# The last microseconds of a one-core decode kernel: output sum turned to five rows, contiguous weight reads, six pieces for the last load

## Chip, cores, metric

The kernel runs on one core of one Trainium2 chip. The metric is the device time of one execution in microseconds (us), as the median of several executions. The profile is one execution taken by the hardware profiler. Its engines are PE (matmul; PEld is its weight load), DVE (VectorE), ACT (ScalarE), POOL and SP. SP mostly issues DMAs here. "L395" is line 395 of that kernel's file.

## The reference

One token passes a layernorm, then attention over a cache of 32 heads x 32768 positions x 128, plus, in parallel, a SwiGLU feed-forward block. All is added to the input:

```python
x  = A_x                                        # [1, 1, 640] bf16
xn = layernorm(x)
return x + attention(xn, k_cache, v_cache, wq, wo) + (silu(xn @ w_gate) * (xn @ w_up)) @ w_down
# k_cache, v_cache: [1, 32, 32768, 128] bf16; wq [640, 4096]; wo [4096, 640]; w_down [1728, 640]
```

The two caches are 537 MB of the 554 MB that the kernel reads.

## The kernel before

SP streams everything through a ring of three SBUF slots: wq, then K and V of each head, then the feed-forward weights, and last wo. At the end PE forms `w_down` and `wo` products in one PSUM tile `acc` of 128 partitions x 5 columns, DVE adds the input, and SP writes 640 values out. These are the parts that the change touches:

```python
D = 640; NCD = 5; OC = 32                      # 32 row blocks of wo, one per 128 rows
WTAIL = [16, 8, 4, 2, 2]                       # row blocks per wo load, a semaphore each
...
wd_v = wd.rearrange("p j (m c) -> p j m c", c=NCD)            # output column = 5*m + c
wo_v = wo.rearrange("p (j m c) -> p j m c", j=OC, c=NCD)
...
# SP, after all K and V, and the feed-forward weights
for i, n in enumerate(WTAIL):
    e.dma_start(wo[:, j * D:(j + n) * D], wo_src[:, j * D:(j + n) * D]).then_inc(s_wo[i], 16)
    j += n
e.wait_ge(s_fin, 1)
e.dma_start(out[0, 0:1, :].rearrange("o (p c) -> (o p) c", c=NCD), outb[:, :]).then_inc(s_out, 16)
...
# PE
def project():
    j = 0
    for i, n in enumerate(WTAIL):
        t.wait_ge(s_wo[i], 16)
        for _ in range(n):
            for c in range(NCD):
                mm = t.matmul(acc[:, c:c + 1], lhsT=wo_v[:, j, :, c], rhs=ot[:, j:j + 1], ...)
            j += 1
...
# DVE
v.wait_ge(s_att, 1)
v.tensor_tensor(out=outb[:, :], in0=xf[:, :], in1=acc, op=ALU.add).then_inc(s_fin, 1)
```

For each row block, five matmuls of one moving column each use a 128x128 piece of the weight as the stationary operand. Column `c` of `acc` holds outputs `5*m + c`, so a weight load reads every fifth element (10 bytes apart), and partition `m` of `outb` holds five neighbouring outputs. The output DMA is therefore 128 runs of 10 bytes.

Of the kernel before, what the change touches and what calls it, by code (L numbers as in the profile page):

```python
# [5 lines left out]
ALU = mybir.AluOpType  # L6
ACTF = mybir.ActivationFunctionType
AX = mybir.AxisListType
BF16 = mybir.dt.bfloat16
F32 = mybir.dt.float32  # L10


def bass_parallel_sum__gqa_block_cached__swiglu_ffn__decode_kernel(
# [18 lines left out]
    NCD = D // 128  # L32
# [14 lines left out]
    TAIL = [128, 64, 32, 32]  # L47
    RB = DH // 32
    OC = H * DH // 128
    WTAIL = [16, 8, 4, 2, 2]  # L50
    PARTS = [64, 64, 128]
    W = 512 // DH
    assert sum(TAIL) == NJ and sum(PARTS) == NJ and NHF == 4 and (H - H0) % PER == 0 and PER % SLOTS == 0
    assert PER % PR == 0 and PER % SR == 0
    assert OC == 32 and H * RB == 128 and sum(WTAIL) == OC
    HA = 5
# [22 lines left out]
    with ExitStack() as es:  # L79
        def sbt(name, shape, dtype):  # L80
            return es.enter_context(nc.sbuf_tensor(name, shape, dtype))

        def sem(name):
            return es.enter_context(nc.semaphore(name))
# [5 lines left out]
        ident = sbt("ident", [128, 128], BF16)  # L90
# [7 lines left out]
        ot = sbt("ot", [128, OC], BF16)  # L98
        hcol = sbt("hcol", [128, FB], BF16)
        sg = sbt("sg", [128, 2, FB], F32)  # L100
        one1 = sbt("one1", [1, 1], BF16)
        xf = sbt("xf", [128, NCD], F32)
        xc = sbt("xc", [128, NCD], F32)
        xq = sbt("xq", [128, NCD], F32)
        xn = sbt("xn", [128, NCD], BF16)
        outb = sbt("outb", [128, NCD], BF16)
# [8 lines left out]
        s_x, s_wq, s_out = sem("x"), sem("wq"), sem("o")  # L115
# [11 lines left out]
        s_exp, s_pv, s_o4, s_fold, s_ov = sem("exp"), sem("pv"), sem("o4"), sem("fold"), sem("ov")  # L127
        s_f, s_fa, s_fd = sem("ffn_pe"), sem("ffn_act"), sem("ffn_dve")
        s_att, s_fin = sem("att"), sem("fin")
        s_ob, s_op, s_ot = sem("o_blocks"), sem("o_ps"), sem("o_rows")  # L130
        block = es.enter_context(nc.Block())

# [3 lines left out]
        xrow = flat[0:1, x0 + NCD * 128:x0 + NCD * 128 + D]  # L136
# [8 lines left out]
        wd = flat[:, d0:d0 + FB * D].rearrange("p (j d) -> p j d", j=FB)  # L145
        assert 2 * NCD * F + FB * D <= CE
        wg_v = wg.rearrange("p (c n) -> p c n", c=NCD)
        wu_v = wu.rearrange("p (c n) -> p c n", c=NCD)
        wd_v = wd.rearrange("p j (m c) -> p j m c", c=NCD)

        def hidden(w, c, j):
            if j < FM:
                return w[:, c, 0:FM * 128].rearrange("p (m j) -> p m j", j=FM)[:, :, j]
            return w[:, c, FM * 128:F]
        wo = flat[:, WO_S * CE:WO_S * CE + OC * D]
        wo_v = wo.rearrange("p (j m c) -> p j m c", j=OC, c=NCD)
        assert OC * D <= CE

        def kv_src(cache, h, j0, n):
# [21 lines left out]
        with nc.psum_tensor("ps8", [128, 8, 512], F32) as ps8:  # L181
# [3 lines left out]
            op = ps8[:, 5, 8:8 + OC]  # L185
            acc = ps8[:, 6, 0:NCD]
            fold_ps = ps8[:, 6, 8:9]
            misc = ps8[:, 7, :]
            ffn = bank[0]

            @block.sync
            def sp(e):
                owner = {}
                for u in units:
                    s = slot_of[u]
                    if s in owner:
                        e.wait_ge(*owner.pop(s))
                    if u[0] == "wq":
                        e.dma_start(wq, A_wq.rearrange("(p c) n -> p (c n)", c=NCD)).then_inc(s_wq, 16)  # L199
                        owner[s] = (s_q, NQB)  # L200
                    elif u[0] == "k":
                        e.dma_start(ring[:, s, :], kv_src(A_k_cache, u[1], 0, NJ)).then_inc(s_slot[s], 16)
                        owner[s] = (s_qk, NHF * (u[1] + 1))
                    elif u == LASTV:
                        j = 0
                        for i, n in enumerate(TAIL):
                            e.dma_start(ring[:, s, j * DH:(j + n) * DH],
                                        kv_src(A_v_cache, u[1], j, n)).then_inc(s_tail[i], 16)
                            j += n
                    elif u[0] == "v":  # L210
                        e.dma_start(ring[:, s, :], kv_src(A_v_cache, u[1], 0, NJ)).then_inc(s_slot[s], 16)
                        owner[s] = (s_pv, u[1] + 1)
                    elif u[0] == "ffn":
                        e.dma_start(wg, B_w_gate.rearrange("(p c) n -> p (c n)", c=NCD)).then_inc(s_ffn[0], 16)
                        e.dma_start(wu, B_w_up.rearrange("(p c) n -> p (c n)", c=NCD)).then_inc(s_ffn[1], 16)
                        e.dma_start(flat[:, d0:d0 + FM * D], B_w_down[0:FM * 128, :].rearrange(
                            "(p j) n -> p (j n)", j=FM)).then_inc(s_ffn[2], 16)
                        e.dma_start(wd[0:FL, FM, :], B_w_down[FM * 128:F, :]).then_inc(s_ffn[2], 16)
                    else:
                        wo_src = A_wo.rearrange("(p j) n -> p (j n)", j=OC)  # L220
                        j = 0
                        for i, n in enumerate(WTAIL):
                            e.dma_start(wo[:, j * D:(j + n) * D], wo_src[:, j * D:(j + n) * D]).then_inc(s_wo[i], 16)
                            j += n
                e.wait_ge(s_fin, 1)
                e.dma_start(out[0, 0:1, :].rearrange("o (p c) -> (o p) c", c=NCD), outb[:, :]).then_inc(s_out, 16)
                e.wait_ge(s_out, 16)

            @block.gpsimd
# [21 lines left out]
            def pe(t):  # L251
# [2 lines left out]
                t.wait_ge(s_a, 2)  # L254
                for c in range(NCD):
                    mm = t.matmul(misc[:, 8 + c:9 + c], lhsT=xrow_v[:, :, c], rhs=one1[:, :], start=True, stop=True)
                mm.then_inc(s_pa, 1)

                t.wait_ge(s_a, 4)
# [6 lines left out]
                for b in range(NQB):  # L266
                    for c in range(NCD):
                        mm = t.matmul(bank[b], lhsT=xnb[:, c, :], rhs=wq_v[:, c, b * 512:(b + 1) * 512],  # L268
                                      start=(c == 0), stop=(c == NCD - 1))
# [108 lines left out]
                def down():  # L378
                    t.wait_ge(s_ffn[2], 32)
                    t.wait_ge(s_fd, 8)  # L380
                    first = True
                    for j in range(FB):
                        n = 128 if j < FM else FL
                        for c in range(NCD):
                            t.matmul(acc[:, c:c + 1], lhsT=wd_v[0:n, j, :, c], rhs=hcol[0:n, j:j + 1],
                                     start=first, stop=False, skip_group_check=True)
                            first = False

# [3 lines that stand above are left out]
                        t.wait_ge(s_wo[i], 16)  # L392
                        for _ in range(n):
                            for c in range(NCD):
                                mm = t.matmul(acc[:, c:c + 1], lhsT=wo_v[:, j, :, c], rhs=ot[:, j:j + 1],  # L395
                                              start=False, stop=(j == OC - 1), skip_group_check=True)
                            j += 1
                    return mm
# [17 lines left out]
                down()  # L416
                t.wait_ge(s_ot, 1)
                project().then_inc(s_att, 1)

            @block.scalar  # L420
            def act(a):
# [54 lines left out]
            def dve(v):  # L476
                n_a = [0]

                def step(ins):
                    ins.then_inc(s_a, 1)  # L480
                    n_a[0] += 1
                    v.wait_ge(s_a, n_a[0])
# [2 lines left out]
                step(v.memset(one1[:, :], 1.0))  # L485
                v.wait_ge(s_pa, 1)
                step(v.tensor_copy(out=xf[:, :], in_=misc[:, 8:8 + NCD]))
                step(v.tensor_reduce(out=st[:, 0:1], in_=xf[:, :], axis=AX.X, op=ALU.add))
                v.wait_ge(s_pa, 2)
                step(v.tensor_scalar(out=st[:, 1:2], in0=misc[:, 0:1], scalar1=1.0 / D, scalar2=None,  # L490
# [56 lines left out]
                with v.Fori(0, (H - H0) // PER) as i:  # L547
                    group[0] = i
                    for h in range(H0, H0 + PER):
# [11 lines left out]
                                in1=blk[:, None, :].to_broadcast([128, H, RB]), op=ALU.mult).then_inc(s_ob, 1)  # L561
                v.wait_ge(s_fa, 2)
                pieces = [(slice(0, 128), slice(0, FM)), (slice(0, FL), slice(FM, FB))]
                n = 0
                for stage in range(4):
                    for p, f in pieces:
                        fu = slice(FB + f.start, FB + f.stop)
                        if stage == 0:
                            ins = v.tensor_scalar(out=sg[p, 0, f], in0=sg[p, 0, f], scalar1=1.0, scalar2=None,
                                                  op0=ALU.add)  # L570
                        elif stage == 1:
                            ins = v.reciprocal(out=sg[p, 1, f], in_=sg[p, 0, f])
                        elif stage == 2:
                            ins = v.tensor_tensor(out=sg[p, 0, f], in0=sg[p, 1, f], in1=ffn[p, f], op=ALU.mult)
                        else:
                            ins = v.tensor_tensor(out=hcol[p, f], in0=sg[p, 0, f], in1=ffn[p, fu], op=ALU.mult)
                        ins.then_inc(s_fd, 1)
                        n += 1
                    v.wait_ge(s_fd, n)
                v.wait_ge(s_att, 1)  # L580
                v.tensor_tensor(out=outb[:, :], in0=xf[:, :], in1=acc, op=ALU.add).then_inc(s_fin, 1)


# [26 lines left out]
```

## Time and profile before

| what | value | where it is read |
|---|---|---|
| time, median of 3 runs at first | 1289.76 us (1289.53 to 1289.88) | the runs |
| span of the profiled run | 1288.2 us | the page |
| bytes, rate | 554.17 MB at 430 GB/s | the page, DMA line |
| PE, DVE busy | 81%, 52% of the span | the page |

The first view is from the page: DMA busy tenths and GB/s in 40 slices, and the sum of the packets.

```profile
DMA  9999999999999999999999999999999999999998
GB/s 421 426 425 446 426 429 442 429 431 440 431 431 433 435 431 429 440 431 431 440 427 431 444 427 431 442 429 431 435 433 433 429 438 433 427 442 431 427 422 340
DMA packets 11182, 554.17 MB, mean 430 GB/s; under 512 B 1377, under 2 KB 1442, under 8 KB 1826
```

DMA reads 9 everywhere but in the last slice. The kernel is bound by its stream of bytes, and no other engine's work can shorten the middle. What is left is what happens before the stream is under way and after its last byte. The timeline shows the end (start in us, duration, engine, line, operation, operands, count; in brackets the idle time before it and what ended it; the lines of PEld are left out, here and below):

```profile
1274.55 3.02 PE L385 MATMUL ps<-hcol,ring 128*128 128x1 bf16 x70 [1.49 <-DVE hcol L576]
...
1277.78 6.76 PE L395 MATMUL ps<-ot,ring 128*128 128x1 bf16 x160 [0.21 <-DMA ring<-in_A_wo_dram]
1284.65 0.16 DVE L581 TENSOR_TENSOR outb<-xf,ps 128x5 bf16<-128x5 f32 x1 [10.24 <-PE ps L395]
1284.84 0.35 SPq L226 DMA_DIRECT2D out_dram<-outb  x1
```

The 160 matmuls of wo (L395) look like one solid block after the first piece landed, 42 ns each. The DMA view gives, per issue, size and time from issue to landing:

```profile
ring<-in_A_wo_dram SPq DMA_DIRECT2D x1, 2560.0 KB, 25.2
ring<-in_A_wo_dram SPq DMA_DIRECT2D x1, 1280.0 KB, 28.1
ring<-in_A_wo_dram SPq DMA_DIRECT2D x1, 640.0 KB, 29.1
ring<-in_A_wo_dram SPq DMA_DIRECT2D x2, 320.0 KB, 29.6
...
out_dram<-outb SPq DMA_DIRECT2D x1, 1.2 KB, 3.0
```

With issues from 1252.43 on, the pieces landed at 1277.64, 1280.94, 1282.38, 1283.15 and 1283.94 us (single semaphore events of the trace). The stream itself ended at 1283.94. The program ended 4.27 us later, and 2.98 us of that is the output of 1.2 KB.

### The profile page before, as it was taken

Reading aid. Unit: us, or ns where it says so; the run is one execution under the profiler, and the core shown is the slowest. Engines: PE = TensorE matmul, PEld = TensorE weight load, DVE = VectorE, ACT = ScalarE, POOL = GpSimd, SP = SyncE. Lnnn points to the kernel's source line nnn. Section 1 sums busy time; section 2 is a strip of 40 time slices with the busy share of each in tenths; the row PEclk is TensorE's granted clock in tenths of the full one; section 3 lists DMA queues with packets and bytes.
Section 4 is the critical chain, followed back from the end, with each engine's and each line's share of the span. In section 5 each row is a group of like instructions: output and inputs, shape, how many; then the busy total and the mean of one; then the engine's idle time right before and its main releaser. Section 6 shows DMA issues by size and latency. Waiting matters only on the chain.

```text
span 1288.2 us, 9847 instructions
## 1 busy us (share of the span) xinstructions
PE 1043.7 (81%) x5148; PEld 263.9 (20%) x3228; DVE 670.0 (52%) x407; ACT 52.2 (4%) x140; POOL 2.5 (0%) x17
## 2 busy tenths in 40 slices
PE   4598778789777788778788777788777788777797
PEld 1011112221112221112221112221112221112237
DVE  0855665445665445664446664446664446664440
ACT  2000000000000000000000000000000000000000
POOL 0000000000000000000000000000000000000000
PEclk9799888898888999888898888898888998888895
DMA  9999999999999999999999999999999999999998
GB/s 421 426 425 446 426 429 442 429 431 440 431 431 433 435 431 429 440 431 431 440 427 431 444 427 431 442 429 431 435 433 433 429 438 433 427 442 431 427 422 340
DMA packets 11182, 554.17 MB, mean 430 GB/s; under 512 B 1377, under 2 KB 1442, under 8 KB 1826
## 3 DMA queue, kind: packets, MB, share of 16 engines
q1 hardware_dynamic: 11168, 554.00, 99.6%
q8 instruction: 9, 0.15, 0.0%
q14 instruction: 3, 0.02, 0.0%
q10 hardware_dynamic: 2, 0.00, 0.0%
HBM read 553.99 MB, written 0.00 MB: 430 GB/s over the span
## 4 chain that ended last, share of the span: by engine, by line
DMA 53%; PE 31%; DVE 11%; issue 6%; DVEq 0%; SPq 0%
DMA ring<-in_A_k_cache_dram 51%; PE ps L308 17%; PE ps L276 11%; DVE ring L522 10%; DMA ring<-in_A_wo_dram 2%; PE ps L295 1%; PE ps L395 1%; PE ps L350 0%; PE ps L344 0%; PE ps L338 0%; DVEq L522 0%; DVE sc L528 0%; DVE pmax L534 0%; SPq L199 0%; DVEq L172 0%
## 5 line engine op out<-in xcount | busy, mean ns | idle before, releaser
L522 DVE TENSOR_TENSOR ring<-ring,qb 128x8192 bf16<-128x8192 bf16 x128 | 557.8, 4419 | 316.4 <-DMA ring<-in_A_k_cache_dram 316.4
L276 PE MATMUL ps<-ring,ident 128*128 128x512 bf16 x1920 | 496.5, 417 | 0.0
L308 PE MATMUL ps<-ring,P 128*4 128x512 bf16 x1984 | 443.3, 379 | 0.0
L295 PE MATMUL ps<-ring,ident 128*128 128x512 bf16 x128 | 55.9, 437 | 220.7 <-DVE ring L522 220.3
L308 PEld LDWEIGHTS ps<-ring,P 128*4 128x4 bf16 x1984 | 163.4, 85 | 237.8
L295 PEld LDWEIGHTS ps<-ring,ident 128*128 128x128 bf16 x128 | 12.6, 99 | 617.5 <-DVE ring L522 344.4
L528 DVE TENSOR_REDUCE sc<-ps 128x64 f32<-128x512 f32 x128 | 82.2, 682 | 63.0 <-PE ps L276 63.0
L540 DVE TENSOR_SCALAR negb<-ps 128x1 f32<-128x1 f32 x32 | 5.1, 158 | 108.4 <-PE ps L350 108.4
L446 ACT ACTIVATE P<-sc,negb 128x256 bf16<-128x256 f32 x32 | 16.2, 508 | 956.7 <-DVE negb L540 956.7
L537 DVE TENSOR_REDUCE m<-ps 1x1 f32<-1x128 f32 x32 | 8.9, 278 | 85.2 <-PE ps L344 85.2
L330 PEld LDWEIGHTS ps<-identf,o 4*128 4x128 f32 x248 | 30.5, 189 | 13.1 <-issue 13.1
L330 PE MATMUL ps<-identf,o 4*128 4x1 f32 x248 | 33.1, 250 | 0.0
L338 PEld LDWEIGHTS ps<-rsum,ones 128*128 128x128 f32 x64 | 12.1, 190 | 99.4 <-issue 98.6
L437 ACT ACTIVATE o<-ps,rzb 4x512 f32<-4x512 f32 x31 | 21.0, 678 | 6.2 <-PE ps L308 6.2
L268 PE MATMUL ps<-ring 128*128 128x512 bf16 x40 | 11.4, 457 | 11.2 <-DMA ring<-in_A_wq_dram 11.2
L442 ACT ACTIVATE ocol<-ps 128x1 f32 (+1 forms) x31 | 5.4, 174 | 222.1 <-PE ps L330 222.1
L534 DVE TENSOR_REDUCE pmax<-sc 128x1 f32<-128x256 f32 x32 | 13.4, 420 | 0.0
L344 PE MATMUL ps<-identf,pmax 128*1 128x128 f32 x64 | 12.2, 273 | 1.2 <-DVE pmax L534 1.2
L350 PE MATMUL ps<-m,ones 1*128 1x1 f32 x64 | 12.1, 256 | 0.4 <-DVE m L537 0.4
L350 PEld LDWEIGHTS ps<-m,ones 1*128 1x128 f32 x64 | 9.4, 182 | 14.2 <-issue 13.5
L374 PE MATMUL ps<-xn,ring 128*128 128x1 bf16 (+1 forms) x140 | 8.9, 198 | 1.4 <-issue 1.4
L510 DVE RECIPROCAL rzb<-ps 128x1 f32<-128x1 f32 x32 | 5.0, 157 | 8.1 <-PE ps L338 8.1
(56 smaller groups left out, 84.9 us busy)
## 6 DMA issues: line engine op xcount, KB each, us to landing
ring<-in_A_wq_dram SPq DMA_DIRECT2D x1, 5120.0 KB, 15.3
ring<-in_A_v_cache_dram SPq DMA_DIRECT2D x1, 4096.0 KB, 31.9
ring<-in_A_wo_dram SPq DMA_DIRECT2D x1, 2560.0 KB, 25.2
ring<-in_B_w_gate_dram SPq DMA_DIRECT2D x1, 2160.0 KB, 22.8
ring<-in_B_w_up_dram SPq DMA_DIRECT2D x1, 2160.0 KB, 27.6
ring<-in_B_w_down_dram SPq DMA_DIRECT2D x1, 2080.0 KB, 31.7
ring<-in_A_v_cache_dram SPq DMA_DIRECT2D x1, 2048.0 KB, 36.4
ring<-in_A_v_cache_dram SPq DMA_DIRECT2D x2, 1024.0 KB, 39.4
```

What stands on the lines that cost most here:

```text
L276: return t.add_instruction(mybir.InstMatmult(start_tensor_calc=False, stop_tensor_calc=stop, tile_size=(128, 128), tile_position=(0, 0), l ...
L295: t.matmul(ob, lhsT=ident[:, :], rhs=src, start=True, stop=False)
L308: mm = t.matmul(O, lhsT=P[:, h % PR, j:j + W], rhs=ring[:, s, j * DH:(j + W) * DH], start=(j == 0), stop=(j + W == NJ))
L330: mm = t.matmul(fold_ps, lhsT=o4[:, m * DH:(m + 1) * DH], rhs=identf[0:W, m:m + 1], start=(m == 0), stop=(m == W - 1))
L344: t.matmul(misc[0:1, 0:128], lhsT=pmax[:, h % SR:h % SR + 1], rhs=identf[:, :], start=True, stop=True).then_inc(s_t, 1)
L350: t.matmul(misc[:, 128:129], lhsT=ones[0:1, :], rhs=m1[0:1, h % SR:h % SR + 1], start=True, stop=True).then_inc(s_b, 1)
L395: mm = t.matmul(acc[:, c:c + 1], lhsT=wo_v[:, j, :, c], rhs=ot[:, j:j + 1], start=False, stop=(j == OC - 1), skip_group_check=True)
L437: a.activation(out=o4[:, :], in_=O, func=ACTF.Copy, scale=rzb[0:W, h % SR:h % SR + 1]).then_inc(s_o4, 1)
L446: a.activation(out=P[:, h % PR, :], in_=sc[:, :], func=ACTF.Exp, bias=negb[:, h % SR:h % SR + 1], scale=c_scale, accum_out=rsum[:, h % SR: ...
L522: v.tensor_tensor(out=kh, in0=kh, in1=q[:, None, :].to_broadcast([128, HF, DH]), op=ALU.mult).then_inc(s_mul, 1)
L528: v.tensor_reduce(out=sc[:, i * HF:(i + 1) * HF], in_=bank[i].rearrange("p (j e) -> p j e", e=G), axis=AX.X, op=ALU.add).then_inc(s_red, 1)
L534: v.tensor_reduce(out=pmax[:, h % SR:h % SR + 1], in_=sc[:, :], axis=AX.X, op=ALU.max).then_inc(s_max, 1)
```

## The change

Its intent is to shorten what follows the last byte of wo. Output column `c*128 + m` now belongs to column `c`, so weight reads are contiguous. The 128x5 sum is turned by a matmul against the identity into 5 rows of 128, so the output is 5 runs of 256 bytes. The last wo load is one row block instead of two. The residual has to be in the same order, hence `xr` beside the layernorm's `xf`.

```diff
-    WTAIL = [16, 8, 4, 2, 2]
+    WTAIL = [8, 8, 8, 5, 2, 1]
...
-        wd_v = wd.rearrange("p j (m c) -> p j m c", c=NCD)
+        wd_v = wd.rearrange("p j (c m) -> p j c m", c=NCD)
-        wo_v = wo.rearrange("p (j m c) -> p j m c", j=OC, c=NCD)
+        wo_v = wo.rearrange("p (j c m) -> p j c m", j=OC, c=NCD)
...                                    (the same index order in the matmuls of w_down and wo)
-                e.wait_ge(s_fin, 1)
-                e.dma_start(out[0, 0:1, :].rearrange("o (p c) -> (o p) c", c=NCD), outb[:, :]).then_inc(s_out, 16)
+                e.wait_ge(s_fin, 2)
+                e.dma_start(out[0, 0:1, :].rearrange("o (c m) -> (o c) m", c=NCD), orow[:, :]).then_inc(s_out, 16)
...                                    (PE, at the start)
+                for c in range(NCD):
+                    mm = t.matmul(misc[:, 16 + c:17 + c], lhsT=xrow[:, c * 128:(c + 1) * 128], rhs=one1[:, :],
+                                  start=True, stop=True)
...                                    (PE, at the end)
+                t.wait_ge(s_fin, 1)
+                t.matmul(orow_ps, lhsT=outb[:, :], rhs=ident[:, :], start=True, stop=True).then_inc(s_or, 1)
...                                    (DVE, at the start)
+                v.tensor_copy(out=xr[:, :], in_=misc[:, 16:16 + NCD]).then_inc(s_xr, 1)
...                                    (DVE, at the end)
-                v.tensor_tensor(out=outb[:, :], in0=xf[:, :], in1=acc, op=ALU.add).then_inc(s_fin, 1)
+                v.tensor_tensor(out=outb[:, :], in0=xr[:, :], in1=acc, op=ALU.add).then_inc(s_fin, 1)
+                v.wait_ge(s_or, 1)
+                v.tensor_copy(out=orow[:, :], in_=orow_ps).then_inc(s_fin, 1)
```

More of the change, by code (lines that the diff above doesn't have):

```diff
@@ L102, in bass_parallel_sum__gqa_block_cached__swiglu_ffn__decode_kernel @@
         xf = sbt("xf", [128, NCD], F32)
+        xr = sbt("xr", [128, NCD], F32)
+        orow = sbt("orow", [NCD, 128], BF16)
         xc = sbt("xc", [128, NCD], F32)
@@ L129, in bass_parallel_sum__gqa_block_cached__swiglu_ffn__decode_kernel @@
         s_att, s_fin = sem("att"), sem("fin")
+        s_xr, s_or = sem("xr"), sem("orow")
         s_ob, s_op, s_ot = sem("o_blocks"), sem("o_ps"), sem("o_rows")
@@ L188, in bass_parallel_sum__gqa_block_cached__swiglu_ffn__decode_kernel @@
             misc = ps8[:, 7, :]
+            orow_ps = ps8[0:NCD, 5, 128:256]
             ffn = bank[0]
@@ L384, in down @@
                         for c in range(NCD):
-                            t.matmul(acc[:, c:c + 1], lhsT=wd_v[0:n, j, :, c], rhs=hcol[0:n, j:j + 1],
+                            t.matmul(acc[:, c:c + 1], lhsT=wd_v[0:n, j, c, :], rhs=hcol[0:n, j:j + 1],
                                      start=first, stop=False, skip_group_check=True)
@@ L394, in project @@
                             for c in range(NCD):
-                                mm = t.matmul(acc[:, c:c + 1], lhsT=wo_v[:, j, :, c], rhs=ot[:, j:j + 1],
+                                mm = t.matmul(acc[:, c:c + 1], lhsT=wo_v[:, j, c, :], rhs=ot[:, j:j + 1],
                                               start=False, stop=(j == OC - 1), skip_group_check=True)
@@ L579, in dve @@
                     v.wait_ge(s_fd, n)
+                v.wait_ge(s_xr, 1)
                 v.wait_ge(s_att, 1)
-                v.tensor_tensor(out=outb[:, :], in0=xf[:, :], in1=acc, op=ALU.add).then_inc(s_fin, 1)
+                v.tensor_tensor(out=outb[:, :], in0=xr[:, :], in1=acc, op=ALU.add).then_inc(s_fin, 1)
+                v.wait_ge(s_or, 1)
+                v.tensor_copy(out=orow[:, :], in_=orow_ps).then_inc(s_fin, 1)
 _INS = ['A_x', 'A_k_cache', 'A_v_cache', 'A_wq', 'A_wo', 'B_x', 'B_w_gate', 'B_w_up', 'B_w_down']
```

## The prediction

> **What bounds the kernel now.** DMA bytes. The page counts 554.17 MB at 430 GB/s over a span of 1288.2 us, and the DMA row reads 9 in all slices but the last (8). PE is 81% busy, DVE 52%. The change leaves these bytes, the per-head loop and its waits alone. Only the two ends can move: the first 16 us, and what follows the last byte of wo.
>
> **The end, before** (timeline, landings, single instructions). The wo pieces land at 1277.64, 1280.94, 1282.38, 1283.15 and 1283.94 us. The projection's 160 matmuls start every 40 ns and wait at piece borders; the last 10 start at about 1283.98, after the last landing. DVE adds at 1284.65 (0.16 us), the output DMA is issued at 1284.84, its sixteen engine completions arrive from 1286.13 to 1287.82, and the program ends 0.34 us later. So 4.2 us follow the last byte of weights: 0.64 to the end of the matmuls, 0.26 for the add, 2.98 for the output DMA, 0.34 for the end.
>
> **What the change does there.**
> 1. Contiguous wo and w_down. At the same half clock, the P·V tail's contiguous weights start every 26.7 ns, these with a step of 5 elements every 40 ns, and the hidden layer with a step of 13 about every 62. The Trainium skill, "SBUF — State Buffer", says that reads crossing to a new 16-byte line pay a penalty; this trace agrees (40 against 26.7 ns). It takes 160 x 13 = 2.1 us off the projection and 0.9 off w_down, but nearly all of that is hidden behind wo's arrival. What counts is after the last landing.
> 2. The last piece is one row, not two: 5 matmuls at 27 ns instead of 10 at 40. That removes about 0.25 us.[...]
> 3. Added in series: a hop to PE (0.1), the identity matmul at half clock with 128 columns (estimated 0.3 from the 0.18 of one column), a hop (0.07), a PSUM copy of 5x128 (0.2 to 0.25; the 1x128 reduce took 0.28). Together +0.6 us before the output is issued.
> 4. The output DMA: 5 runs of 256 bytes instead of 128 of 10 bytes. Before, the first engine completed 1.29 us after issue, the last 2.98. The Trainium skill, "DMA: Bandwidth & Descriptors", section on why a semaphore rises by 16, says that only engines that carry a part complete through data; here 5 instead of 16. I expect all at 1.3 to 1.9 us, so -1.1 to -1.7.
>
> Sum: -0.2 + 0.6 - 1.4, about -1.0 us, all on the critical path.
>
> **The start.** Five more matmuls and a copy delay the layernorm by 0.3 us; its result is ready at about 6.8 us and the first wq matmul waits for DMA until 16.1. Free.
>
> **Predicted:** 1288.8 us, range 1287.9 to 1289.9. Faster by over 2%: 0.005; within 2%: 0.99; slower by over 2%: 0.005.
>
> **What would show it.** In the groups, wo and w_down matmuls at 27 ns spacing, with gaps at each landing; last wo landing still between 1283.8 and 1284.1; output issued at about 1285.3; its completion under 1.9 us after issue instead of 2.98; first wq matmul still at 16.1.
>
> **What would make it wrong.** Five 256-byte writes that also complete only after 2.5 to 3 us (if the write's round trip, not the number of engines, makes the tail): then the change costs 0.4 us. A matmul-copy hop much over 0.6 us. A last landing that moves with the DMA rate from run to run, 0.1% of which is 1.3 us and as large as the effect. Shifted small tiles that slow the per-head chain, which should not show while DMA is full.

## The result, and the profile after

The changed kernel took 1288.71 us (median of 4 runs, 1288.56 to 1288.99), the kernel before in the same rounds 1289.82 us (4 runs, 1289.53 to 1290.09). The ratio is 0.9992, with an interval of 0.9974 to 1.0009. It is the mean time of one kernel's runs over that of the other's of the same rounds, so not quite the ratio of the medians. By that interval the verdict is "same". Still, 1.1 us less is a real shift. All runs of the changed kernel, including four more (1288.68 to 1288.75), lie below the fastest of all 25 runs of the kernel before (1289.53).

The timeline of the changed kernel's end:

```profile
1274.31 2.10 PE L392 MATMUL ps<-hcol,ring 128*128 128x1 bf16 x70 [1.49 <-DVE hcol L586]
...
1276.34 2.58 PE L402 MATMUL ps<-ot,ring 128*128 128x1 bf16 x80
1280.77 1.45 PE L402 MATMUL ps<-ot,ring 128*128 128x1 bf16 x40 [1.84 <-DMA ring<-in_A_wo_dram]
1282.75 1.47 PE L402 MATMUL ps<-ot,ring 128*128 128x1 bf16 x40 [0.53 <-DMA ring<-in_A_wo_dram]
1284.36 0.16 DVE L592 TENSOR_TENSOR outb<-xr,ps 128x5 bf16<-128x5 f32 x1 [10.19 <-PE ps L402]
1284.57 0.27 PE L427 MATMUL ps<-ident,outb 128*5 128x128 bf16 x1 [0.35 <-DVE outb L592]
1284.88 0.28 DVE L594 CAST orow<-ps 5x128 bf16<-5x128 f32 x1 [0.36 <-PE ps L427]
1285.19 0.36 SPq L230 DMA_DIRECT2D out_dram<-orow  x1
```

Three things are to be seen. The 70 matmuls of w_down take 2.10 us where they took 3.02. The wo block now has holes of 1.84 and 0.53 us in which PE waits for DMA, so PE has caught up with the stream. And the output is issued later than before, 1285.19 against 1284.84, because of the two steps L427 and L594. The DMA view, for the sizes of the pieces:

```profile
ring<-in_A_wo_dram SPq DMA_DIRECT2D x3, 1280.0 KB, 25.0
ring<-in_A_wo_dram SPq DMA_DIRECT2D x1, 800.0 KB, 29.1
ring<-in_A_wo_dram SPq DMA_DIRECT2D x1, 320.0 KB, 29.4
ring<-in_A_wo_dram SPq DMA_DIRECT2D x1, 160.0 KB, 28.9
```

The last piece landed at 1283.88 us, against 1283.94 before, so the stream is the same. The span is 1286.8 us. The following table cuts the time after the last wo landing into its steps, from single events of each trace, in us. The experiments below use the same cut.

| step | before | after |
|---|---|---|
| last wo landing to start of the add | 0.71 | 0.47 |
| the add | 0.16 | 0.16 |
| add's end to issue of the output | 0.03 | 0.67 |
| issue to last completion | 2.98 | 1.19 |
| last completion to end | 0.39 | 0.40 |
| sum | 4.27 | 2.89 |

At the start, the new copies delay the layernorm, as the timelines of both show (before, then after):

```profile
5.97 0.82 DVE L503 COPY ring<-xn 128x640 bf16<-128x640 bf16 x1
16.14 11.40 PE L268 MATMUL ps<-ring 128*128 128x512 bf16 x40 [11.24 <-DMA ring<-in_A_wq_dram]
```

```profile
6.16 0.82 DVE L513 COPY ring<-xn 128x640 bf16<-128x640 bf16 x1
16.26 1.01 PE L275 MATMUL ps<-ring 128*128 128x512 bf16 x2 [11.17 <-DMA ring<-in_A_wq_dram]
```

The layernorm's result comes 0.19 us later and still waits some 9 us for wq, so this costs nothing. (The second line of the after view is cut by the window at 17 us, hence x2.)

### The profile page after: what moved, and what is told of

It is laid out like the page before. It is cut to its first block, busy times and chain, and to the rows that moved or that the text cites. A ratio compares the mean times of both kernels' runs of the same rounds, so it can differ in the third digit from the quotient of the medians.

```text
span 1286.8 us, 9861 instructions
## 1 busy us (share of the span) xinstructions
PE 1044.2 (81%) x5153; PEld 261.3 (20%) x3234; DVE 670.3 (52%) x409; ACT 52.2 (4%) x140; POOL 2.5 (0%) x17
## 4 chain that ended last, share of the span: by engine, by line
DMA 53%; PE 30%; DVE 11%; issue 6%; SPq 0%; DVEq 0%
DMA ring<-in_A_k_cache_dram 51%; PE ps L315 17%; PE ps L283 11%; DVE ring L532 10%; DMA ring<-in_A_wo_dram 2%; PE ps L302 1%; PE ps L357 0%; PE ps L351 0%; PE ps L345 0%; PE ps L402 0%; SPq L227 0%; DVEq L532 0%; DVE sc L538 0%; DVE pmax L544 0%; SPq L203 0%
```

## The experiments

Theory A is the prediction's: the gain is the output DMA's shorter completion, less the turn, plus about 0.2 us from the matmuls after the last landing. Rival B is that the wo side (smaller last piece, contiguous reads) carries the gain. Rival C is drift of the load stream between runs. A second question is why the old output took 3 us: the number of engines, as the prediction said, or something else.

### One part of the change at a time

**Pieces alone**: the kernel before with

```diff
-    WTAIL = [16, 8, 4, 2, 2]
+    WTAIL = [8, 8, 8, 5, 2, 1]
```

> The kernel before with only the six wo pieces 8,8,8,5,2,1. Theory A (the gain of about 1.1 us is the output DMA's 1.8 us less 0.65 us for the turn, and 0.2 us of the matmuls after the last landing): the last five matmuls at 40 ns in place of ten save 0.2 us between the last landing and the add, the output DMA still takes about 3.0 us, so 1289.6 us against 1289.8. Rival B (the gain comes from wo: smaller last piece and contiguous reads): about half of the gain, 1289.2. Rival C (drift of the load rate between builds or runs): anything within 0.5 us, with the last wo landing moved by as much as the time.

Measured: correct, 1289.86 us (4 runs, 1289.70 to 1290.20), the kernel before 1289.62 in the same rounds. There was no gain. Landing to add (the first row of the table above) took 0.74 us, not less than the 0.71 before, so theory A's 0.2 us was wrong for this kernel. The timeline shows why:

```profile
1280.78 1.76 PE L395 MATMUL ps<-ot,ring 128*128 128x1 bf16 x40 [0.20 <-DMA ring<-in_A_wo_dram]
1282.73 1.76 PE L395 MATMUL ps<-ot,ring 128*128 128x1 bf16 x40 [0.20 <-DMA ring<-in_A_wo_dram]
1284.60 0.16 DVE L581 TENSOR_TENSOR outb<-xf,ps 128x5 bf16<-128x5 f32 x1 [10.48 <-PE ps L395]
```

The piece of five landed at 1282.69. From there 40 matmuls at 40 ns need 1.6 us, while the last piece was there after 1.17 us (1283.86). Twelve matmuls started after the last landing, not five. PE still had a backlog when the last byte came, so the size of the last piece did not matter.

**Old pieces in the changed kernel**: the reverse edit of the one above, in the changed kernel.

> The changed kernel with the five old pieces 16,8,4,2,2. Theory A: ten contiguous matmuls after the last landing instead of five, 0.13 us more[...]; 1288.8 us. Rival B: at least 0.4 us of the gain is lost, 1289.1 or more.

Measured: correct, 1288.88 us (4 runs, 1288.55 to 1288.88). Landing to add 0.61 us, that is 0.13 us more than with the new pieces, as theory A said.

```profile
1284.12 0.42 PE L402 MATMUL ps<-ot,ring 128*128 128x1 bf16 x10 [0.35 <-DMA ring<-in_A_wo_dram]
1284.68 0.16 DVE L592 TENSOR_TENSOR outb<-xr,ps 128x5 bf16<-128x5 f32 x1 [9.62 <-PE ps L402]
```

The timeline of this run shows that PE waited 0.35 us for the last piece and then had ten matmuls left. Here the size of the piece is what counts.

**Old read step in the changed kernel** (the output comes out permuted, and so wrong):

```diff
-        wd_v = wd.rearrange("p j (c m) -> p j c m", c=NCD)
+        wd_v = wd.rearrange("p j (m c) -> p j c m", c=NCD)
-        wo_v = wo.rearrange("p (j c m) -> p j c m", j=OC, c=NCD)
+        wo_v = wo.rearrange("p (j m c) -> p j c m", j=OC, c=NCD)
```

> The changed kernel with the weight reads of w_down and wo at the old step of 5 elements (the output is then a permuted and so wrong result, on purpose; the work is the same). Theory A: matmuls start every 40 ns again, but all except those after the last landing are hidden, so 5 x 13 ns = 0.07 us is lost: 1288.8 us. Rival B: if the reads carry the gain, 0.5 us or more comes back, 1289.2 or more.

Measured: 1289.09 us (4 runs, 1288.86 to 1289.48). Landing to add 0.75 us, a loss of 0.27 and not 0.07:

```profile
1283.39 1.76 PE L402 MATMUL ps<-ot,ring 128*128 128x1 bf16 x40 [0.18 <-DMA ring<-in_A_wo_dram]
1285.28 0.16 DVE L592 TENSOR_TENSOR outb<-xr,ps 128x5 bf16<-128x5 f32 x1 [11.12 <-PE ps L402]
```

In the profiled run the last piece also landed late, at 1284.53, so only intervals are compared. With the two runs above this makes a table of landing to add:

| us | pieces 16,8,4,2,2 | pieces 8,8,8,5,2,1 |
|---|---|---|
| read step 5 | 0.71 (before) | 0.74 (pieces alone), 0.75 (old read step) |
| contiguous | 0.61 (old pieces) | 0.47 (changed) |

The two edits do not add up as separate gains. Contiguous reads alone give 0.10, smaller pieces alone give nothing, and together they give 0.24. Faster reads let PE catch up with the stream, and only then is the last piece what is left. Rival B's part is real but small, 0.24 us.

**No turn**: the changed kernel with the output sent straight from the 128x5 tile (its order is then wrong):

```diff
-                e.wait_ge(s_fin, 2)
-                e.dma_start(out[0, 0:1, :].rearrange("o (c m) -> (o c) m", c=NCD), orow[:, :]).then_inc(s_out, 16)
+                e.wait_ge(s_fin, 1)
+                e.dma_start(out[0, 0:1, :].rearrange("o (p c) -> (o p) c", c=NCD), outb[:, :]).then_inc(s_out, 16)
                 (the identity matmul and the copy to orow are taken out)
```

> The changed kernel without the turn: the sum goes out straight as 128 runs of 10 bytes, as before (with the contiguous weights this order of the output is wrong, on purpose). Theory A: output issued about 0.65 us sooner than in the changed kernel, but complete only about 3.0 us after issue instead of 1.2; in all 1.15 us slower than the changed kernel, 1289.5 to 1289.9. Rivals B and C: within 0.3 us of the changed kernel, or faster by the hop of 0.65 us that is gone.

Measured: 1289.52 us (4 runs, 1289.47 to 1289.68). That is 0.8 us over the changed kernel's 1288.71. It lies in the expected range of times, though the difference is smaller than the expected 1.15, as its output completed sooner than the expected 3.0 us. It was run at another time. The end of its timeline:

```profile
1284.82 0.16 DVE L590 TENSOR_TENSOR outb<-xr,ps 128x5 bf16<-128x5 f32 x1 [10.43 <-PE ps L402]
1285.01 0.35 SPq L230 DMA_DIRECT2D out_dram<-outb  x1
```

and its DMA view:

```profile
out_dram<-outb SPq DMA_DIRECT2D x1, 1.2 KB, 2.5
```

The output was issued 0.03 us after the add, and its last completion came 2.49 us later. Landing to end is 3.56 us against 2.89 with the turn. So the turn, which puts 0.64 us of work in series, pays for itself through the output DMA alone, and rival B falls as the main cause.

**The changed kernel again**, beside the kernel before:

> The changed kernel once more, on the same chip and rounds as the version before it in this call: 1288.7 us by every theory that does not put the gain down to the chip it ran on; last wo landing to end 2.9 us; output complete 1.18 us after issue.

Measured: correct, 1288.72 us (4 runs, 1288.68 to 1288.75), the kernel before 1289.83. Landing to end was 2.90 us, and the output was complete 1.19 us after issue. The gain is no accident. Single executions do drift: the last landing lay between 1283.86 and 1284.53 us in the twelve traces whose loads at the start are the same. But before and after it differs by 0.06 us only, and the times of the two kernels do not overlap in 8 and 25 runs, so rival C falls.

### Why the old output took 3 us

The prediction gave the number of engines as the reason. Four runs change the shape of the output DMA, and before it only the copy that feeds it and what that copy needs. The first has few engines and many small runs, the second many engines with one run each (wrong result):

```diff
 few engines, small runs: the row buffer padded, right result
-        orow = sbt("orow", [NCD, 128], BF16)
+        orow = sbt("orow", [NCD, 16, 16], BF16)           # 8 of each 16 used: runs of 16 bytes
 sixteen engines: 16 partitions of 80 bytes, 11 rows of the turned sum are zero
-        outb = sbt("outb", [128, NCD], BF16)
+        outb = sbt("outb", [128, 16], BF16)
```

> The changed kernel with the output row buffer padded so that the output DMA is 5 partitions of 16 runs of 16 bytes: few engines, 80 small runs, right result. If the long completion of the old output (2.5 to 3.0 us after issue) comes from having sixteen engines share it, this completes in about 1.2 to 1.4 us like the 5 runs of 256 bytes. If it comes from small writes to memory, it completes in 2.3 us or more.

> The changed kernel with 16 partitions of 80 bytes as the output (11 of the 16 rows hold zeros: a wrong result on purpose): sixteen engines, one run each. If the engine count makes the tail, it completes in 2.3 us or more with sixteen spread completions; if the many 10-byte writes do, in about 1.2 to 1.5 us.

Measured: the small runs completed 2.20 us after issue (one execution, 1289.94 us, correct), the sixteen engines after 1.38 us (one execution, 1289.08 us). They were run on another chip.

The timelines have the issues, of the small runs and then of the sixteen engines (start, time of the issue):

```profile
1285.54 0.97 SPq L230 DMA_DIRECT2D out_dram<-orow  x1
```

```profile
1285.51 0.36 SPq L230 DMA_DIRECT2D out_dram<-orow  x1
```

Sixteen engines are not the cause: with one run each they complete only 0.19 us after the five. For the small runs the total time alone would have misled me. Their issue took 0.97 us instead of 0.36, their first packet came 1.56 us after the start of issue instead of 0.78, and from the last packet on they were as quick as any. The tail has to be read from the end of the last packet. So the next two kernels kept the 10-byte runs of the old output, but gave each engine a stretch of its own (both with a wrong result):

```diff
-        orow = sbt("orow", [NCD, 128], BF16)
+        orow = sbt("orow", [16, 8, 8], BF16)              # 5 of each 8 used: 8 runs of 10 bytes per partition
+        orow = sbt("orow", [4, 32, 8], BF16)              # the other kernel: 32 runs of 10 bytes
```

> The changed kernel with the output sent from 16 partitions as 8 runs of 10 bytes each (a wrong result on purpose): the same 128 runs of 10 bytes on sixteen engines as the old output, but each engine's 80 bytes are one stretch of the output. Read: last completion after the last packet has ended (old output 1.45 to 1.95 us, 5 runs of 256 bytes 0.33, 80 runs of 16 bytes 0.36). If engines that write into each other's neighbourhood make the tail, this is under 0.7 us; if the 10-byte runs themselves do, it is 1.2 us or more. The issue itself is likely to take longer, as with the runs of 16 bytes.

> The same with 4 partitions of 32 runs of 10 bytes (wrong result on purpose): four engines, each alone in its 320 bytes, so no two engines come near each other. If the tail needs several engines in one stretch, the last completion comes under 0.6 us after the last packet; if it comes from runs of 10 bytes as such, 1.2 us or more.

Measured (one execution each, 1291.18 and 1290.98 us), in us from the start of issue, from the trace's packets and semaphore events, with the earlier runs beside them:

| output as | first packet | last packet ended | last completion | tail after last packet |
|---|---|---|---|---|
| 128 x 10 B (before) | 0.84 | 1.04 | 2.98 | 1.94 |
| 128 x 10 B (pieces alone) | 0.84 | 1.04 | 2.85 | 1.81 |
| 128 x 10 B (no turn) | 0.85 | 1.05 | 2.49 | 1.45 |
| 16 partitions x 8 runs of 10 B | 1.35 | 1.59 | 3.73 | 2.14 |
| 4 partitions x 32 runs of 10 B | 1.43 | 2.05 | 3.41 | 1.36 |
| 5 partitions x 16 runs of 16 B | 1.56 | 1.84 | 2.20 | 0.36 |
| 16 partitions x 80 B | 0.86 | 1.02 | 1.38 | 0.37 |
| 5 partitions x 256 B (after) | 0.78 | 0.86 | 1.19 | 0.33 |
| 4 partitions x 320 B (rows without a turn, below) | 1.23 | 1.31 | 1.64 | 0.33 |

All five rows with 10-byte runs have a tail of 1.36 to 2.14 us, whether 16 engines interleave, 16 engines have a stretch each, or 4 engines are far apart. All four with runs of 16, 80, 256 or 320 bytes have 0.33 to 0.37, with 4, 5 or 16 partitions and with 1 or 16 runs each. The tail goes with the 10-byte runs. It is spent after the last packet's record has ended, so moving the bytes is not what takes long. What stays open is whether it is the length of 10 bytes, the start at a multiple of 10, which is not a multiple of 4 or 16, or the number of runs, which is 128 in all five slow rows and at most 80 in the quick ones; no run separates these.

### The half clock, and a version without a turn

In both kernels PE's granted clock fell to half at 1257 us and stayed there to the end. **Idle work to keep it up**:

```diff
+                def warm(n):
+                    for _ in range(n):
+                        t.matmul(bank[1], lhsT=ident[:, :], rhs=qb[:, 0:512], start=True, stop=True)
...              (3 before w_down's wait, and 2, 4 and 1 before the second, third and fourth piece of wo)
```

> The changed kernel with ten idle 128x512 matmuls put into the gaps of PE's wait for wo, to see what the half clock costs at the end. If they bring the clock back to full before the last wo piece lands, [...]0.15 to 0.2 us less after the last landing. If the clock stays at half, the time is that of the changed kernel, or up to 0.1 us more.

Measured: correct, 1289.89 us (4 runs, 1289.12 to 1290.11): a loss of 1.2 us. It was run on another chip. The windows view of this run (stretch and its length in us, PE busy, its matmuls, granted clock, DMA share, GB/s):

```profile
1272.00:1274.00 2.00, 2.00 (x29) 0.50 1.01 420
1274.00:1276.00 2.00, 2.00 (x39) 0.50 0.99 415
1276.00:1278.00 2.00, 2.00 (x74) 0.50 1.01 425
1278.00:1280.00 2.00, 2.00 (x51) 0.50 1.00 410
1280.00:1282.00 2.00, 1.03 (x11) 0.50 0.96 388
1282.00:1284.00 2.00, 2.00 (x44) 0.50 0.45 166
```

The clock stayed at 0.50 through 8 us of solid PE records, so this run does not measure what the full clock would be worth. The trace of the kernel before says something of it: the contiguous one-column matmuls at the end of its attention (P·V, L320) start every 25 ns before 1257 us, at full clock, and every 26.7 ns after, at half. By this the five matmuls after the last landing would gain an estimated 0.01 us (5 x 1.7 ns). The idle matmuls, up to 427 ns apart, put PE behind the stream: landing to add grew to 1.45 us. The loss was a miss: at most 0.1 us had been expected. Nor did all idle work fill gaps. PE's records pause for 0.97 us up to 1281.14, and the four idle matmuls meant for the wait before the third piece started only at 1281.22, after it had landed at 1281.19. The profile names nothing that ended this pause.

**Rows without a turn.** Here the weights move and the vectors stand still, so the sum comes out as four rows of 160:

```diff
-                            t.matmul(acc[:, c:c + 1], lhsT=wd_v[0:n, j, c, :], rhs=hcol[0:n, j:j + 1], ...)
+                            t.matmul(orow_ps[32 * g:32 * g + 32, :], lhsT=hcol[0:n, j:j + 1].to_broadcast([n, 32]),
+                                     rhs=wd[0:n, j, g * 160:(g + 1) * 160], ...)       # g = 0..3; wo alike
+                    a.dma_start(xr[32 * g:32 * g + 32, :],
+                                A_x[0, 0:1, 160 * g:160 * (g + 1)].to_broadcast([32, 160])).then_inc(s_xr, 16)
-  ... orow[:, :] from the turn
+                e.dma_start(out[0, 0:1, :].rearrange("o (g m) -> (o g) m", g=4), orow[0:128:32, :]).then_inc(s_out, 16)
```

> The changed kernel with w_down and wo as the moving operand: four matmuls of 160 columns for each row block, into PSUM partitions 0, 32, 64 and 96, so that the sum already lies in four rows, without a turn. The output is 4 runs of 320 bytes. After the last matmul one add of 160 columns (about 0.32 us) in place of add and turn (0.83 us). If the four column groups run at the same time or PE goes to full clock, PE keeps up with the wo landings (0.39 us a row) and the program is about 0.5 us shorter than the changed kernel: 1288.2. If they run one after another at half clock (0.53 us a row), PE ends several us after the last landing: 1292 or more.

Measured: correct, 1289.44 us (4 runs, 1289.05 to 1289.72), slower than the changed kernel by 0.7 us, where 0.5 us less had been expected. It was run on another chip. The end of its timeline:

```profile
1281.68 1.26 PE L398 MATMUL ps<-ring,ot 128*32 128x160 bf16 x32 [1.85 <-DMA ring<-in_A_wo_dram]
1283.65 1.51 PE L398 MATMUL ps<-ring,ot 128*32 128x160 bf16 x32 [0.72 <-DMA ring<-in_A_wo_dram]
1285.31 0.32 DVE L589 TENSOR_TENSOR orow<-xr,ps 128x160 bf16<-128x160 bf16 x1 [10.88 <-PE ps L398]
1285.66 0.63 SPq L230 DMA_DIRECT2D out_dram<-orow  x1
```

The idea worked where it was in doubt. The four matmuls of a row block start within 14 ns of each other and each block takes 133 ns at half clock, so PE waits for the stream as before. From last landing to issue it took 0.87 us against 1.30. Two things gave it all back. The issue of four rows with a partition step of 32 took 0.63 us, and completion came 1.64 us after its start instead of 1.19, so that landing to end was 2.91 us against 2.89. And the last landing itself came at 1284.79, 0.9 us late. The stream was late from its beginning: 5 MB had arrived at 15.42 us instead of 14.74 in the changed kernel, and 50 MB at 119.54 instead of 118.75 (sums over the packets). The DMA view of the first 5 us shows what is new there:

```profile
ring<-in_A_wq_dram SPq DMA_DIRECT2D x1, 5120.0 KB, 15.9
xr<-in_A_x_dram ACTq DMA_DIRECT2D x4, 10.0 KB, 15.2
```

The four loads that copy the input to 32 partitions each run beside wq. In the twelve traces without these loads 50 MB had arrived at 118.73 to 119.03 us, and in the other kernel with them, the next one, at 119.26. That they are the cause is argued from this, and not isolated by a run.

**The same with two output transfers**, two rows from SP's queue and two from ACT's:

```diff
-  e.dma_start(out[0, 0:1, :]..., orow[0:128:32, :]).then_inc(s_out, 16)
+  e.dma_start(out[0, 0:1, 0:320].rearrange("o (g m) -> (o g) m", g=2), orow[0:64:32, :]).then_inc(s_out, 16)
+  a.dma_start(out[0, 0:1, 320:640].rearrange("o (g m) -> (o g) m", g=2), orow[64:128:32, :]).then_inc(s_o2, 16)
```

> The version with w_down and wo as moving operand, its output split into two transfers of 2 rows, from SP's and from ACT's queue. There one transfer of 4 rows with a partition step of 32 took 0.63 us to issue, its first packet came 1.23 us after the start of issue (0.78 in the changed kernel), and it completed at 1.64. If the cost of issue goes with the rows of that step, two rows complete at about 1.4 us, and last wo landing to end is about 2.6 us against 2.9 in the changed kernel; if not, about 2.9 and no gain.

Measured: correct, 1289.74 us (4 runs, 1289.46 to 1290.01). This was a miss. Each issue took 0.6 us even for two rows, the later completion came at 1.84 us, and landing to end was 3.17 us. No version that I ran beats the changed kernel.

This trace shows one thing more: PE's granted clock was full again from 1279.3 to 1282.8 us. Just before, from 1276.0 to 1279.3, PE was busy for 3.15 us with 92 matmuls of 160 columns. In the kernel before, 3.40 us of PE records without a gap (1267.3 to 1270.7), nearly all of one column, brought nothing. That the number of columns makes the difference is a guess from one trace.

## Why the prediction was right or wrong

- **Time.** 1288.8 was predicted, 1288.71 measured. The predicted sum, -0.2 + 0.6 - 1.4 = -1.0 us, stands against -1.1 of the medians, and against -0.24 + 0.64 - 1.79 = -1.39 after the last landing in the two profiled runs. These two lie apart: the one before took 1290.1 us, 0.28 over its median, and the one after 1288.56, 0.15 under its own. The 10-byte output also varies, 2.49 to 2.98 us in the traces of three kernels, and the kernel before had the longest. How much of the 0.3 us each of these explains is not shown. That the sum came so close is in part luck: its largest term was drawn from a wrong cause.
- **What bounds the kernel, and the start.** Right: the stream kept its rate, the first wq matmul still waited for DMA (16.26 us).
- **Last landing.** Right: 1283.88, inside 1283.8 to 1284.1. What the extra DMA costs is not visible among the run-to-run changes of that landing.
- **Contiguous reads and the small piece.** The size was right (0.24 measured for "about 0.25"), and the spacing of 27 ns too. In the changed kernel five matmuls do follow the last landing, and ten in the kernel before, as item 2 says. What failed is the split of this gain between pieces and reads, in item 2 (it puts all of it under the last piece) and in what I expected of the runs. It took PE as level with the stream in all versions. With reads at 40 ns and the new pieces it is not: twelve matmuls are left, and the small piece is worth nothing (0.74 against 0.71). The reads are then worth 0.27, not the 0.07 that I expected of the run. The Trainium skill, "SBUF — State Buffer", in its section on the DMA port swizzle, says that consecutive accesses to one 16-byte line run at full bandwidth and that crossing to a new line has a penalty. The trace agrees in direction: 26.7 ns contiguous, 40 at a step of 10 bytes, at the same clock.
- **The turn.** Right: +0.6 predicted, 0.67 - 0.03 = 0.64 measured, of which matmul 0.27 and copy 0.28.
- **The output DMA.** Mis-sized and for a wrong reason. I expected completion after 1.3 to 1.9 us, so a gain of 1.1 to 1.7; it was 1.19, a gain of 1.79 between the profiled runs. The reason given, 5 engines instead of 16, fell: sixteen engines with 80 bytes each complete in 1.38 us, and four engines with 10-byte runs have a tail of 1.36 us. In its place the runs show a tail that goes with the 128 runs of 10 bytes, 1.36 to 2.14 us against 0.33 to 0.37. What the Trainium skill, "DMA: Bandwidth & Descriptors", in its section on why a semaphore rises by 16, says of the count is borne out: the changed output shows five late events and one at 0.47 us, the old one sixteen. But it says who completes, not how long that takes, and I drew a time from it.

## What to carry to other kernels

In a kernel that is bound by its stream of bytes, cut the time after the last landing into steps (work left, hops, issue, packets, completion) before you change it, for that is where small changes count. Write a small output in few, longer runs: here a turn of 0.64 us (a matmul, a copy and their hops) was worth it to get rid of 128 runs of 10 bytes. A smaller last piece pays only if the engine that consumes the stream has caught up with it when that piece lands, so make the consumer faster first.

## What the Trainium skill lacked or had wrong

- "DMA: Bandwidth & Descriptors" says that below 512 bytes a transfer does read-modify-write, and does not tell small writes apart. Here runs of 16, 80, 256 and 320 bytes to HBM completed 0.33 to 0.37 us after the last packet, runs of 10 bytes 1.36 to 2.14 us.
- The same page, in its account of the other issuing path (SWDGE), calls descriptor generation "small, variable". For SP's path it does not say how the cost goes with the pattern. Here the issue took 0.35 us for 128 x 10 bytes and 0.36 for 5 x 256 bytes, but 0.97 for 5 x 16 runs of 16 bytes, and 0.63 for four rows with a partition step of 32. No page that I read has the cost of such patterns.
- The fixed cost of about 2.0 us on that page is for the other issuing path (SWDGE). A 1.2 KB output issued from SP completed in 1.19 us here.
- "TensorE: Matmul & The Clock Gate" says that full clock comes after one busy window of about 3.4 us. Here PE's records were solid for 8 us (one-column matmuls with some of 512 columns between) and the clock stayed at half; in one other run it came back after 3.15 us of 160-column matmuls. Except for transposes, the page does not say which work counts.
- The same page's section on weight-path modes lists strided weight reads beside packed ones without a cost. At half clock a 128x128 bf16 weight started every 26.7 ns when contiguous and every 40 ns at a step of 5 elements.
